# A gated pair of long convolutions on one core: gate sums in four column groups, eight unsummed Q rows, and the output stored in two parts

## The chip, the core and the metric

The kernel runs on one core of a Trainium2 chip. It uses five engines: TensorE (PE; its weight loads are listed apart as PEld), VectorE (DVE), ScalarE (ACT), GpSimd (POOL) and SyncE (SP), which here only issues transfers; ACT issues some too. The metric is device time in microseconds (us). Three timed runs of the kernel before gave 301.37, 303.55 and 303.87 us: a median of 303.55.

## The reference, cut to what matters

```python
x = A_u                                              # 2048 steps, 448 channels
g = sigmoid((x * gate_w).sum(-1, keepdims=True))     # one gate for each step
a = A_ref(x, A_re, A_im, B_re, B_im, C_re, C_im, log_dt, Dskip)
b = B_ref(x, k, v, shift_k, ssm_k, ssm_D)
return g * a + (1 - g) * b

# A: dt = exp(log_dt); K[d,l] = Re sum_n C[d,n] * exp(dt*A[d,n]*l) * dt*B[d,n], n < 256, l < 2048
#    y = causal convolution of x with K (by an FFT of length 4096) + x * Dskip
# B: kv = v * (k passed through a shift filter of 4 taps)
#    y = q * (causal convolution of kv with ssm_k + kv * ssm_D), with q = x
```

Inputs and output are bf16; both convolutions are per channel.

## The kernel before, in words

**Layout.** The 448 channels lie as 4 groups g of 112, the 2048 steps as 32 (a) by 64 (b). A natural tile such as `uu` (the input u), `vt`, `kt` or `ug` (the output) has 128 partitions (g, a) and 64 x 112 elements: partition 32g + a holds steps (a, b) of the channels of group g. The 112 channels are handled in 4 quarters H of 28 (`NC`), and each quarter of kernel generation in 2 blocks of 14 (`CB`), so 8 blocks j.

**Convolutions** are FFTs made of matmuls with generated twiddle tables: `spread` (first stage, PSUM tile `ps_c`, tables `Wc`, `WcK`), `transform` (second stage, `ps_2`, shown as `ps`, table `s_W`), a product in the frequency domain on DVE (`products`: `zs`, and the half-swapped copy `zsS`, which a DMA makes), then back by `stage_a` (`ps_a`, table `sa_R`) into `U` and by `stage_b` (`ps_b`, table `sb_G`). Between the stages ACT copies PSUM into SBUF (`evac`). The eight convolutions run in the order B0, B1, B2, A0, B3, A1, A2, A3.

**The SSM kernel K** is generated block by block (`KGen.block`, lines 398 to 464). exp(dt·A·l) with l = 8q' + ... is split into powers for Q rows (tile `kg_TQ`, 21 rows, `NQ`) and P columns (`kg_TP`, 32). Each level multiplies the rows it has by a unit phasor from table `ET`: `mult` makes the four real products of each complex multiplication into `kg_P4` (shown as `kg_P`) with one DVE instruction, and `add` sums them in pairs into `kg_TQ` or `kg_TP` with another. `pk` matmuls (224 for a block, in four column groups, weights `kg_TQ`, moving `kg_TP`) sum over the modes; ACT copies the result to `kg_S`; `ps_g` matmuls pick the right Q row for each l with 0/1 weights `ga_sel`, which `Consts.rows` and `Consts.gather` (lines 251 to 305) build from a table of row numbers; ACT copies the result to `kg_KT`, and `spread` takes it on. `kg_TQ` has two buffers, `kg_TP` one. Block 7's last products are done by halves (`transform_half`, `last`, `stage_a_half`).

**The gate.** `gwt` holds the gate weights, each times a 32-wide one-hot of the partition's a. 112 matmuls (line 917), one per channel of a group, add up into `ps_gate` (64 x 32): weights are `uu[:, :, l]` (128 x 64, stride 112), moving is `gwt[:, l, :]`. ACT copies the sums four times over into `gx`, PE transposes, ACT takes a tanh, DVE makes `gt` (g), `gb` (g in bf16) and `og` (1 − g).

**The end.** `mix` (line 867) scales the finished quarters of `ug` by 1 − g (`ug<-ug,og`) and of `uu`, which by then holds the A outputs (`uu<-uu,gb`), and adds them (`ug<-ug,uu`). For the last quarter `epilogue_A` multiplies each 16-b part of `ps_b` by g (`ept`), adds it to `ug`, and `store` (line 844) sends that quarter of b with all 112 channels to DRAM: 4 transfers, two on SP's queue and two on ACT's, 16 in all, each of 512 runs of 224 bytes.

**Order.** Nothing is scheduled by a planner's costs. Every instruction is first recorded (`Listed`, `Order`) and then issued in the order of the string `ORDER`, a list of record numbers; line 146 issues them all, so that the profile gives nearly every instruction line 146, and the groups are told apart by tile names. On each engine the instructions run in that order. Constants are carved from `scratch`, a tile that shares its buffer with `kg_TP`. Semaphores are added where one instruction needs another's result or buffer; transfers on the hardware queues take one of eight completion semaphores in turn, and an issue first waits for the earlier transfer with the same one.

Of the kernel before, what the change touches and what calls it, by code (L numbers as in the profile page):

```python
# [31 lines left out]
NQ = 21  # L32
# [9 lines left out]
    "600 25 576 30 164 1 190 525 24 36 188 196 162 189 175 177 23 34 186 191-192 187 176 193 526 534 26 31 552 173 "  # L42
    "171 580 174 536 581 0 32 160 593 537 2 166 172 528 33 73 535 598 21 179 17 35 540 11 10 14 3 22 28 75 16 6 182 "
    "178 13 18 12 29 15 7 19 198 184 9 38 591 8 5 20 4 37 181 74 65 180 183 39 76 201 27 161 550 197 577 168 200 167 "
    "41 542 163 544 589 169 165 194 79 590 40 582 170 541 195 42 599 583 52 199 185 202 586 592 69 584 587 585 588 "
    "100 46-47 203 50 72 51 553 44 595 204 594 551 43 538 48 45 110 66 49 557 68 77 101-108 90 53 78 55 554 71 56 539 "
    "150 54 596 63 556 111-118 67 109 62 597 70 527 91-98 555 80 61 64 119 529 140 531 151-158 99 530 234-241 602 545 "
    "130 141-148 159 242 215-222 543 532 120 149 225-232 548 205-212 223 233 213 267 214 549 243-250 224 252-259 547 "
    "251 81-88 533 546 260 121-128 89 319-326 129 262 268-283 261 327 131-138 284 264 263 285-300 139 266 302-317 265 "
    "301 575 516 499 318 493 1104 366 574 469 346-353 486 365 1106 1103 354 367 1105 471 502 470 364 474 473 472 468 "  # L50
    "481 370-385 490 573 477 570 498 562 578 507 567 489 513 561 482 560 494 815-830 483 512 478 579 479 495 484 487 "
    "491 496 488 480 492 485 503 603-616 521 497 522 504 1121 524 523 500 508 505 514 1108 617-630 501 509 517 1110 "
    "506 1109 631-644 510 518 1111 511 645-658 1119 558 1112 1122 1113 659-672 568 1117 673-686 572 559 1115 475 2483 "
    "687-700 566 515 563 1118 571 565 701-714 1124 831 1120 386 60 57-58 1126 798-813 1114 59 715 476 421-428 564 "
    "1123 716 814 1116 1107 1125 429 1510-1517 1846 717 1127 569 1476-1491 1518 2514 328-335 2498 1492 2515 781-796 "
    "519 1847 2497 2489 1848 718 404-419 2488 1129 520 720 1131 2487 719 1128 2491 2486 2492 2485 1133 797 1130 1132 "
    "420 1459-1474 1136 601 336 772-779 1135 1475 337-344 2490 1134 387-402 345 1137 2484 1849 832-839 780 1138 403 "
    "355-362 1850 840 1331-1362 1851 363 1267-1330 2499 1852 369 430-437 448-455 439-446 1853 368 1139-1202 1854 456 "
    "2518 2500 447 2519 1857 1203-1266 1856 2516 1855 438 946-953 2517 2509 1363 1860 1859 2510 1862 2511 1858 "
    "457-464 2520 755-770 2512 954 2521 1382-1421 2506 2502 465 1864 1493-1508 2505 2503 1422 1844 467 937-944 2507 "  # L60
    "1364-1380 1842 2504 1843 1381 1841 1509 1432-1439 2508 2538 2513 2494 721-736 2537 771 2493 2539 466 2495 "
    "738-753 737 754 2496 1639-1646 2533 2532 2540 2501 858-873 2558 2529 945 2528 2557 1861 1845 2522 901-908 2559 "
    "874 1863 1865 909 928-935 1867 1869 1647 2560 892-899 1871 936 2561 910-917 1866 900 919-926 918 1870 955-962 "
    "927 841-856 1868 2530 1872 1455 1648-1655 963 2563 1456 857 875-890 2531 2523 2565 1656 964-971 2524 2568 891 "
    "1873 1440 1038-1101 1874 2534 2525 1875 972 1441-1446 2535 1876 2552 1457 2069-2100 1877-1940 2544 2553-2554 "
    "2546 2005-2068 2549 1102 2545 2555 2550 1941-2004 2536 1458 2548 1447 2543 2541 2556 2551 3326 2547 1448-1453 "
    "2526 1613-1628 2542 2570-2571 2101 3328 3963 3327 2527 2573 1666-1673 1454 2562 1629 1657-1664 1423-1430 1674 "
    "2575 1579-1594 2564 1665 2566 1519-1534 2567 1595 3329 973-1036 3999 3966 3990 3965 3989 3970 3998 3330 3968 "
    "2569 3967 2197-2212 3972 1037 3964 1431 3971 2120-2159 2572 2213 1570-1577 6189 2160 1596-1611 1578 3331 1535 "
    "2102-2118 2574 1536-1551 3969 3333 2119 2577 1612 1630-1637 2186-2191 1552 2576 1553-1568 2579 1638 2578 "  # L70
    "2995-3002 1569 2585 2214-2229 3003 2193-2194 3332 2248-2255 2230-2246 2584 2256 1684-1691 3991 1711-1774 3334 "
    "2586 3335 2247 2581 1692-1700 3974 3973 2583 2192 2944-2959 1701 1775 2170-2178 1702-1709 2580 2960 2587 "
    "2161-2168 1675-1682 1710 3992 2961-2976 3336 1683 2582 3338 2716-2779 2977 3337 2196 2652-2715 2169 3975-3976 "
    "3985-3986 2195 2179-2184 3987 2588-2651 2185 2780-2811 3994 2812 2257-2272 3339 3995 3340 3996 3988 3342 3993 "
    "3978 4000 3344 3977 2317-2324 3350 2273 2335-2342 2813-2829 3979 4001 2308-2315 3983 2830 3352 2325 2831-2870 "
    "3341 4003 2316 3343 2915-2922 4004 2343 3345 2326-2333 3997 2871 1776-1839 3347 2334 3982 3349 3346 4005 2923 "
    "4013 3055-3062 4006 4002 2890-2895 1840 2291-2306 4007 3063 3351 6192 3984 2978-2993 3021-3036 2307 4018 4017 "
    "2994 2274-2289 4012 4019 3348 3037 3980 2924-2931 3353 3981 2344-2351 2290 3354 2352 3728-3735 3355 4029 4020 "
    "2904 2906-2913 3356 2905 4038 3549-3580 4037 4028 4008 4032 4039 4048 4026 3421-3484 4040 4021 4033 4009 4023 "
    "4041 3357-3420 4030 4042 4010 4044 3736 4046 3485-3548 2914 4047 4011 4014 4049 2418-2481 2932 4050-4051 4807 "  # L80
    "4806 4025 4053 4808 4055 4052 4022 4015 4031 2353-2416 4054 4016 2482 4036 4034 4027 4057 4024 3677-3692 3581 "
    "2896 2417 4035 5383 2933-2940 3693 4059 2897-2902 3038-3053 6195 2941 3711-3726 4065 2903 3054 3694-3709 2943 "
    "3727 2872-2879 5388 5392 5384 5393 5387 5406 2942 5386 5389 2880 5385 2881-2888 5391 5390 3710 5405 3115-3122 "
    "5394 4043 2889 3806-3813 5395 4809 3098-3113 4045 4810 4064 3600-3639 3123 3814-3822 5396 4066 3114 3081-3096 "
    "5418 4811 3640 3824-3831 3823 4056 3582-3598 4813 3097 3004-3019 4058 5419 3599 4060 3124-3131 4061 3832 "
    "3650-3657 3132 4062 3064-3079 4063 3658 4817 4067 3142-3149 5407 3666-3671 3080 4815 4132-4195 3672 5415 4816 "
    "3150 3641-3648 5414 4196-4259 4818 3649 5408 5416 4821 3020 5398 4823 5397 4825 5399 3659-3664 4260-4291 5417 "
    "3665 4068-4131 5400 4827 5401 5403 5402 4404-4411 4292 4820 4819 4822 5404 3169-3176 4412 4812 5420 4395-4402 "
    "4824 4293-4309 3177 4814 3151-3158 4826 4310 3133-3140 3159 4311-4350 4830 3141 3160-3167 5421 4351 4832 3673 "
    "3196-3259 3168 5428 5438 3674 5429 4403 5437 4828 5430 3178-3185 5439-5440 4377-4382 3260 4834 4475-4482 "  # L90
    "3186-3194 5458 5409 5424 5449 4833 3261-3324 4829 4835 5451 5455 4831 4836 5452 5456 5454 3195 5431 5029-5060 "
    "5423 5410 4965-5028 5444 3676 5442 5448 5443 3797-3804 3325 4901-4964 5453 6190 5447 5446 5445 5441 3675 5450 "
    "4727-4742 3805 5422 4837-4900 4384 4483 6191 5425 4458-4473 4385 5468 5844-5846 5471 5061 5457 5426 5411 "
    "3788-3795 5470 5459 4474 5473 5460 3796 3754-3769 5412 4383 5461 5413 5432-5433 4352-4359 5475 5427 5462 3770 "
    "4413-4421 5466 4386-4393 5464 4360 3737-3752 4394 5467 5847 4370-4375 5434 3771-3786 4423 3753 4376 4744-4759 "
    "3787 4422 4361-4368 4743 4710-4725 4760 3833-3896 5848 4726 5469 5435 5472 4369 4424-4439 3897 5463 4441-4456 "
    "4440 5474 5465 5062-5078 4535-4542 5436 5476 5079 4518-4533 5481 4543 4457 5080-5119 5478 4484-4499 5483 4534 "
    "5477 4544-4551 5120 4501-4516 4500 5479 5485 5121-5128 4552 4761-4768 4517 5484 3898-3961 4769 5480 5486 5129 "
# [60 lines left out]
class Consts:  # L159
# [31 lines left out]
    def onehot(self, name, n, col, scale=1.0, pool=None):  # L191
        t = (pool or self.pool).tile([P, n], f32, name=name)
        self.nc.vector.tensor_scalar(out=t[:], in0=self.iota(name + "_j", [[1, n]]), scalar1=col[:, 0:1],
                                     scalar2=scale, op0=ALU.is_equal, op1=ALU.mult)
        return t
# [788 lines left out]
```

## Time and profile before

| | |
|---|---|
| median of three runs | 303.55 us |
| profiled execution, its own time | 302.91 us |
| its span | 300.7 us |
| busy: PE, PEld | 224.0, 197.8 us |
| busy: DVE, ACT, POOL | 268.4, 257.7, 9.7 us |
| mean granted TensorE clock | 0.861 |
| last write of `kg_TP` (DVE) ends | 260.7 us |
| last `zs` product (DVE) ends | 282.0 us |
| last `ug` sum (DVE) ends | 290.8 us |
| packets moved by DMA | 53380, of which 48720 under 512 bytes |

Times inside the profile count from the span's start. A group line reads: source line, engine, operation, output<-inputs, partitions x elements, xcount | busy us, mean ns of one | idle time of the engine just before them, and what ended it. In the page's slices each digit is the busy share of a fortieth of the span in tenths, 9 being 90% or more. DVE instructions overlap a little, so that the time from one to the next is shorter than the duration of one.

### The profile page before, as it was taken

The page shows a single profiled execution, that of the slowest core. Times are in us where ns is not written, and L with a number is a line of the kernel's source. Part 1 is how long each engine was busy: PE and PEld are TensorE (multiplying, and loading weights), DVE is VectorE, ACT ScalarE, POOL GpSimd, SP SyncE. Part 2 cuts the span into 40 slices and gives each one's busy share as a digit, 9 for nine tenths or more (in the row PEclk, how much of TensorE's full clock was granted, in tenths as well). Part 3 has the DMA queues.
Part 4 walks back from the last instruction along what each step waited for, and adds up shares of the span by engine and source line. Part 5 has one row for each costly group of instructions (what it writes and reads, how often), then busy time and mean ns, then how long its engine had stood idle before and what let it go on. Part 6 is the DMA issues. An engine that isn't in the chain of part 4 may idle for free.

```text
span 300.7 us, 12051 instructions
## 1 busy us (share of the span) xinstructions
PE 224.0 (74%) x5386; PEld 197.8 (66%) x5386; DVE 268.4 (89%) x536; ACT 257.7 (86%) x413; POOL 9.7 (3%) x42
## 2 busy tenths in 40 slices
PE   0186664997956867998887696978869999869740
PEld 0033444996954766997777685867759988769730
DVE  8999999987987989899999999989999999983850
ACT  4899989979979999899799999999999999906600
POOL 6003000010000000000000000000000000000000
PEclk9999795557689797997999777999788999969995
DMA  6999999210234051040001410005050000900058
GB/s 126 185 216 168 175 154 282 43 23 0 49 80 63 0 125 50 2 104 25 5 2 34 95 49 2 2 5 121 7 124 2 2 4 20 220 17 4 3 112 134
DMA packets 53380, 21.34 MB, mean 71 GB/s; under 512 B 48720, under 2 KB 51664, under 8 KB 53328
## 3 DMA queue, kind: packets, MB, share of 16 engines
q1 hardware_dynamic: 48768, 19.42, 34.6%
q10 hardware_dynamic: 4560, 1.15, 2.0%
q8 instruction: 42, 0.69, 1.0%
q14 instruction: 10, 0.08, 0.1%
HBM read 10.01 MB, written 3.21 MB: 44 GB/s over the span
## 4 chain that ended last, share of the span: by engine, by line
ACT 34%; DVE 16%; PE 9%; issue 3%; DMA 2%; DVEq 0%; ACTq 0%; SPq 0%
ACT zs L146 13%; ACT ET L146 6%; ACT U L146 5%; ACT zsK L146 5%; DVE kg_P L146 4%; PE ps_a L146 3%; DVE kg_TP L146 3%; DMA zsS<-zs 2%; DVE zs L146 2%; ACT L146 2%; DVE ug L146 2%; DVE zsS L146 2%; PE ps_b L146 1%; PE ps_c L146 1%; PE pk L146 1%
## 5 line engine op out<-in xcount | busy, mean ns | idle before, releaser
L146 ACT CAST zs<-ps 128x896 bf16<-128x896 f32 x48 | 43.5, 935 | 1.2 <-PE ps L146 1.2
L146 DVE TENSOR_TENSOR kg_P<-kg_TQ,ET 128x896 bf16<-128x896 bf16 (+2 forms) x64 | 43.9, 705 | 0.6 <-ACT ET L146 0.4
L146 ACT CAST zs<-ps_c 128x1024 bf16<-128x1024 f32 (+1 forms) x48 | 42.4, 925 | 0.8 <-PE ps_c L146 0.8
L146 PEld LDWEIGHTS <-s_W 128*128 128x128 bf16 x544 | 32.7, 107 | 14.7 <-issue 12.2
L146 PE MATMUL ps_a<-sa_R,zs 128*128 128x128 bf16 x224 | 35.6, 245 | 5.0 <-ACT zs L146 3.6
L146 PE MATMUL ps<-zs,s_W 128*128 128x112 bf16 x384 | 30.0, 233 | 9.3 <-ACT zs L146 7.9
L146 PE MATMUL pk<-kg_TP,kg_TQ 128*21 128x32 bf16 x1792 | 30.9, 238 | 7.7 <-issue 5.1
L146 PE MATMUL ps_a<-sa_R,zsS 128*128 128x128 bf16 x224 | 34.9, 243 | 0.7 <-DVE zsS L146 0.7
L146 PEld LDWEIGHTS <-zsS 128*128 128x128 bf16 x224 | 30.8, 154 | 5.7 <-issue 4.2
L146 PEld LDWEIGHTS <-kg_TQ 128*21 128x21 bf16 x1792 | 27.8, 121 | 9.9 <-issue 8.3
L146 PE MATMUL ps_b<-U,sb_G 128*128 128x28 bf16 x1024 | 28.3, 176 | 6.1 <-ACT U L146 2.5
L146 DVE TENSOR_TENSOR kg_P<-kg_TP,ET 128x1792 bf16<-128x1792 bf16 (+1 forms) x32 | 30.7, 968 | 1.8 <-ACT ET L146 1.8
L146 PEld LDWEIGHTS <-sb_G 128*128 128x128 bf16 x1024 | 27.6, 97 | 7.1 <-issue 5.6
L146 PEld LDWEIGHTS <-zs 128*128 128x128 bf16 x224 | 30.7, 153 | 2.4 <-DVE zs L146 0.8
L146 ACT CAST U<-ps_a 128x1024 bf16<-128x1024 f32 (+2 forms) x30 | 28.3, 947 | 3.3 <-PE ps_a L146 3.2
L146 PEld LDWEIGHTS <-uu 128*64 128x64 bf16 x336 | 28.1, 212 | 3.4 <-DMA skraw<-in_B_ssm_k_dram 2.2
L146 DVE TENSOR_TENSOR kg_TQ<-kg_P 128x896 bf16<-128x896 bf16 (+2 forms) x64 | 27.3, 441 | 0.1
L146 ACT ACTIVATE ET<-ks_ph 128x448 bf16<-128x448 int16 x40 | 22.8, 595 | 1.6 <-DVE ks_ph L146 1.6
L146 PEld LDWEIGHTS <-scratch 128*128 128x128 bf16 x65 | 7.2, 112 | 25.0 <-DVE oA_f L146 10.8
L146 ACT ACT_TABLE_LOAD x15 | 19.2, 1283 | 4.3 <-DMA kt<-in_B_k_dram 4.0
L146 ACT CAST zsK<-ps_c 128x512 bf16<-128x512 f32 (+2 forms) x27 | 20.9, 779 | 0.7 <-PE ps_c L146 0.7
L146 DVE TENSOR_TENSOR kg_TP<-kg_P 128x896 bf16<-128x896 bf16 (+2 forms) x40 | 19.8, 500 | 0.0
(132 smaller groups left out, 455.5 us busy)
## 6 DMA issues: line engine op xcount, KB each, us to landing
zsS<-zs SPq DMA_DIRECT2D x16, 448.0 KB, 4.3
kt<-in_B_k_dram SPq DMA_DIRECT2D x16, 112.0 KB, 4.1
skraw<-in_B_ssm_k_dram SPq DMA_DIRECT2D x16, 112.0 KB, 4.4
vt<-in_B_v_dram SPq DMA_DIRECT2D x4, 448.0 KB, 7.1
uu<-in_A_u_dram SPq DMA_DIRECT2D x4, 448.0 KB, 5.9
xfd<-ks_hold SPq DMA_DIRECT2D x2, 672.0 KB, 6.2
ks_xf<-xfd SPq DMA_DIRECT2D x3, 336.0 KB, 2.9
out_dram<-ug SPq DMA_DIRECT2D x8, 112.0 KB, 4.7
```

Of the source, the lines that this page charges most:

```text
L146: ins = f(*args, **kw)
```

## The change

Five things are changed.

1. **Q rows of exponent 1.** The four rows that came from multiplying rows 0 to 3 by the phasor of exponent 1 are no longer summed. `leaf` writes the two products of each real and imaginary part into two rows of `kg_TQ` (rows 17 to 24), with two DVE instructions in place of one product and one sum. `kg_TQ` has 25 rows; the rows are renumbered, and `ga_sel` gets two ones where a row is a pair (`q_half`: the row number is replaced by min(q, (q + 17) >> 1)), so that the `ps_g` matmul adds the pair.
2. **Gate sums.** Weights and moving operand change places: weights `gwt[:, l, :]` (128 x 32), moving `uu[:, :, l]` (64 columns), in four column groups by l mod 4. A matmul with a 128 x 128 matrix of ones at equal a, in `gx`, adds the four groups and copies to all partitions, in place of the transpose.
3. **Stores.** At the end of `mix` the first 84 channels of each group are stored for all b: 4 transfers on SP's queue, each of 2048 runs of 168 bytes. The last epilogue stores the other 28 channels: 16 transfers as before, each of 512 runs of 56 bytes.
4. **Buffers.** Small constants that had tiles of their own are carved from `scratch`, and `ept` takes the buffer of `kg_KT`.
5. **`ORDER`** is a new list throughout, so instructions move on every engine.

```diff
-NQ = 21
+NQ = 25
...
 ORDER = (
-    "600 25 576 30 164 1 190 525 24 36 188 196 162 189 175 177 23 34 186 191-192 187 176 193 526 534 26 31 552 173 "
+    ...
...
+        def named(q):
+            return q if q < 4 else q + 13 if q < 8 else q - 4
...
+        def leaf(dst, src, e):
+            r, m = EQ[:, entry_of(e) + 1], src.shape[1]
+            for c in range(2):
+                V.tensor_tensor(out=TQ[:, dst + c:dst + c + 2 * m - 1:2], in0=src[:, :, c].unsqueeze(2).to_broadcast([P, m, 2, M]),
+                                in1=bass.AP(r.tensor, r.offset + c * M, [list(r.ap[0]), [0, m], [-M, 2], [1, M]]), op=ALU.mult)
...
-        q1 = mult([TQ[:, 0:4]], 1)
-        add(TQ, 8, q256)
-        add(TQ, 4, q1)
+        leaf(17, TQ[:, 0:4], 1)
+        add(TQ, 4, q256)
...
-    cons.gather(cons.field("q1", 0, 31), maskg)
+    q_col, q_half = cons.field("q1", 0, 31), cons.carve(1)
+    V.tensor_scalar(out=q_half, in0=cons.pidx[:], scalar1=31, scalar2=None, op0=ALU.bitwise_and)
+    V.tensor_scalar(out=q_half, in0=q_half, scalar1=17.0, scalar2=None, op0=ALU.add)
+    V.tensor_scalar(out=q_half, in0=q_half, scalar1=1, scalar2=None, op0=ALU.logical_shift_right)
+    V.tensor_tensor(out=q_col[:], in0=q_col[:], in1=q_half, op=ALU.min)
+    cons.gather(q_col, maskg)
...
-    def store(b0, n):
+    def store(b0, n, c0, c1, queues):
         for g in range(4):
-            dmae[g % 2].dma_start(out4[g][:, b0:b0 + n, :], ug[g * 32:(g + 1) * 32, b0:b0 + n, :])
+            queues[g % 2].dma_start(out4[g][:, b0:b0 + n, c0:c1], ug[g * 32:(g + 1) * 32, b0:b0 + n, c0:c1])
...
-            t = kgp.tile([P, 32, NC], bf16, name="ept")[:, 0:n]
+            t = kgp.tile([P, 32, NC], bf16, name="ept", tag="kg_KT")[:, 0:n]
...
-            store(b0, n)
+            store(b0, n, 3 * NC, 112, dmae)
...
                 V.tensor_tensor(out=o, in0=o, in1=x, op=ALU.add)
+        store(0, 64, 0, 3 * NC, (nc.sync, nc.sync))
...
-    V.tensor_copy(gx[:, 0:64], ident[:, 0:64])
+    V.tensor_scalar(out=gx[:, 64:192], in0=cons.iota("four_j", [[0, 4], [1, 32]]), scalar1=a1[:, 0:1], scalar2=None, op0=ALU.is_equal)
...
-        nc.tensor.matmul(pg[0:64, 0:32], lhsT=uu[:, :, l], rhs=gwt[:, l, :], start=(l == 0), stop=(l == 111))
-    nc.scalar.copy(gx[0:64, 64:192].rearrange("p (g a) -> p g a", g=4), pg[0:64, 0:32].unsqueeze(1).to_broadcast([64, 4, 32]))
-    nc.tensor.transpose(out=pg[:, 128:192], in_=gx[0:64, 64:192], identity=gx[0:64, 0:64])
+        q = 32 * (l % 4)
+        nc.tensor.matmul(pg[q:q + 32, 0:64], lhsT=gwt[:, l, :], rhs=uu[:, :, l], start=(l < 4), stop=(l >= 108), tile_position=(0, q))
+    nc.scalar.copy(gx[:, 0:64], pg[:, 0:64])
+    nc.tensor.matmul(pg[:, 128:192], lhsT=gx[:, 64:192], rhs=gx[:, 0:64], start=True, stop=True)
```

Counted from the two instruction lists: DVE has 8 products `kg_P<-kg_TQ,ET` of 128x1792 and 8 sums `kg_TQ<-kg_P` of 128x896 fewer, and 16 products `kg_TQ<-kg_TQ,ET` of 128x896 more. ACT has 13 table loads in place of 15. PE has as many matmuls as before. In the new order the halves of the last convolution stand differently on PE: the 28 `ps_a` matmuls of its first half, which stood ahead of the last `ps_c<-WcK`, stand at the end beside the 28 of the second; the `ps` matmuls of the first half, which stood ahead of the last `pk`, stand behind it. On DVE the last `uu<-uu,gb` and `ug<-ug,uu` stand ahead of the two `U` copies that precede the first `ept`.

## The prediction

> **What bounds the kernel now.** I read the busy shares first, then the 40 slices, then the stretches by engine, and last the end of the timeline. Busy shares and slices, from the page:
>
> ```profile
> span 300.7 us, 12051 instructions
> PE 224.0 (74%) x5386; PEld 197.8 (66%) x5386; DVE 268.4 (89%) x536; ACT 257.7 (86%) x413; POOL 9.7 (3%) x42
> DVE  8999999987987989899999999989999999983850
> ACT  4899989979979999899799999999999999906600
> DMA  6999999210234051040001410005050000900058
> ```
>
> Up to slice 35 (about 262 us) DVE and ACT are both nearly full: no engine alone is the bound, and a saving counts only as far as the other has one too. After that both have holes (a chain through PE), and the last slice and a half have no engine at all, only DMA. So I cost three pieces: the double-bound body up to the last write of `kg_TP` (DVE ends it at 260.7), the chain to the last output, and the stores.
>
> The body has one soft spot. Stretches of 2 us (columns: stretch, busy PE, PEld, DVE, ACT, POOL, granted clock, DMA):
>
> ```profile
> 62.00:64.00 2.00, 2.00 (x19) 2.00 (x18) 2.00 (x4) 1.28 (x2) 1.30 (x1) 0.50 0.00 0
> 64.00:66.00 2.00, 2.00 (x30) 2.00 (x30) 2.00 (x6) 0.83 (x3) 0.00 (x0) 0.50 0.00 0
> 66.00:68.00 2.00, 1.69 (x24) 1.47 (x23) 0.82 (x4) 1.85 (x5) 0.00 (x0) 0.50 0.05 12
> 68.00:70.00 2.00, 2.00 (x31) 1.66 (x26) 1.56 (x8) 1.73 (x4) 0.00 (x0) 0.50 0.00 0
> 70.00:72.00 2.00, 1.75 (x30) 1.63 (x28) 1.12 (x2) 2.00 (x8) 0.00 (x0) 0.91 0.00 0
> ```
>
> At a granted clock of 0.50 PE is full with the gate sums while ACT, and then DVE, stand still. Groups that the change touches (columns: busy, mean ns of one, idle before):
>
> ```profile
> L146 PE MATMUL ps_gate<-gwt,uu 128*64 128x32 bf16 x112 | 13.3, 277 | 2.0 <-ACT ET L146 2.0
> L146 PE MATMUL pk<-kg_TP,kg_TQ 128*21 128x32 bf16 x1792 | 30.9, 238 | 7.7 <-issue 5.1 <-DVE kg_TP L146 2.6
> L146 DVE TENSOR_TENSOR kg_P<-kg_TQ,ET 128x1792 bf16<-128x1792 bf16 x16 | 17.3, 1084 | 0.5 <-ACT ET L146 0.4
> L146 DVE TENSOR_TENSOR kg_TQ<-kg_P 128x896 bf16<-128x896 bf16 x24 | 14.6, 616 | 0.0
> L146 ACT ACT_TABLE_LOAD x15 | 19.2, 1283 | 4.3 <-DMA kt<-in_B_k_dram 4.0
> ```
>
> **Part 1, unsummed Q rows.** Each of 8 blocks loses one 128x1792 product and one 128x896 sum and gains two 128x896 products. Neighbouring DVE instructions overlap by about 0.08 us, so I take the pitch: 1.00 and 0.54 us. Saved: 8 × (1.00 + 0.54 − 2 × 0.54) = 3.7 us. The new products read runs of 112 elements; the sum row reads the same runs at 616 ns, so I give them its price. Bounds: nothing saved if one costs 0.77 us; at 1.00 us it is a loss of 3.7. The extra matmul columns (25 for 21) ride in weight loads: 21 columns cost 121 ns, 32 columns of `ga_sel` 99 ns, so nothing. Small constants on DVE: five more one-column instructions at 0.07 us and the new `gx` (0.15 for 0.20) cost +0.3 us, most of it before 12 us, where DVE is full. The saving reaches the body's end only if ACT gets shorter by as much; part 2 counts that.
>
> **Part 2, the new written order.** Counted from both instruction lists and priced by the rows of before: DVE has 246.2 us of work ahead of its last `kg_TP` write, and 242.6 after the change. ACT has 245.2 us ahead of its last `kg_S` copy, and 240.8: two table loads fewer (13 for 15, 2 × 1.28) and four 128x448 `zsK` copies (4 × 0.49) put behind it. DVE now idles 260.7 − 246.2 = 14.5 us up to that point. If that stays, the body is 3.6 us shorter, and ACT (−4.4) allows it. The order of every queue changes, so the idle time may move; the two lists put each block's `pk` within a few us of the same place in DVE's and ACT's work, so I keep 14.5, with ±2.
>
> **Part 3, gate sums.** 112 matmuls take 13.1 us (51.7 to 64.8), one each 0.118 us. After: weights 128x32 in four column groups, 64 moving columns. Bounds: the `pk` row in four groups runs 128 in 2.10 us (16 ns each, 32 moving columns), the `ps_c<-Wc,kv` row in two groups 32 in 2.24 us (70 ns, 128 moving), both at clock 0.50. So 1.8 to 7.8 us; I take 33 ns, twice `pk`, since the moving side doubles: 3.7 us. Either way the sums end before ACT has done the 23 `ET` pieces that stand ahead of the `gx` copy; ACT no longer waits 1.8 us there. Idle in 60–72 us is 2.7 us on DVE and 2.3 on ACT. What is late next is ACT's `ET` chain, whose exponents DVE awaits anyway, so I count half: −1.3 us (0 to −2.7).
>
> The `pk` row's 16 ns has weight loads and matmuls of different column groups overlapping over the same 128 rows. [...]
>
> **Part 4, stores.** The end of before (timeline; then the DMA share over the stretch):
>
> ```profile
> 284.67 1.08 DVE L146 TENSOR_TENSOR ug<-ug,uu 128x1792 bf16<-128x1792 bf16 x1
> ...
> 290.42 0.39 DVE L146 TENSOR_TENSOR ug<-ept,ug 128x448 bf16<-128x448 bf16 x1
> ```
>
> ```profile
> 287.37 8.53 SPq L146 DMA_DIRECT2D out_dram<-ug  x8
> ```
>
> ```profile
> 288.00:298.50 10.50, 0.67 (x27) 0.57 (x23) 2.50 (x6) 0.00 (x0) 0.00 (x0) 0.70 1.00 174
> 58.00:61.50 3.50, 3.50 (x32) 3.50 (x31) 3.30 (x7) 3.49 (x11) 0.00 (x0) 0.50 0.86 131
> ```
>
> The stores are bound by DMA: 8192 runs of 224 B fill 16 engines for 10.5 us, 20.5 ns a run. `skraw`, 3584 runs of 128 B, costs 0.86 × 3.5 × 16 / 3584 = 13.4 ns. The line through both gives 16.4 ns for 168 B and 8.1 for 56 B. The change makes **8192 early runs of 168 B and 8192 late ones of 56 B**: more DMA work, 12.5 us, so it gains only by starting early. But the early store waits for the last `ug<-ug,uu`, still almost the last thing before the final sums.
>
> Count from t0, the last `zs` product (282.04 before). Before: first `ept` at 4.3, data done at 16.5, span end at 18.7. After: DVE does `uu`, `ug` (2.2 us: early store issued), two `U` copies (2.2), `ps_b` (1.0): first `ept` at 5.4, last `ug` at 9.9. Early data start 0.9 later (issue 287.37, flow from about 288.2) and need 8.4, with the first late quarter's 1.0 between: the last early store lands at 2.2 + 0.9 + 9.4 + 0.6 = 13.1. **Added wait:** a DMA takes one of eight semaphores in turn and its issue waits for that semaphore's earlier user. By the instruction list the second late quarter waits for the early stores and the fourth for the second; queued behind are only further stores. At 2.7 us from issue to landing (small loads show 2.9, less run cost) quarter two's last lands at 15.8, quarter four's at 18.5, span end 1.6 later: 20.1, or +1.4. Ahead of t0, PE has 14 `ps_a` fewer (56 for 70) and 16 short `ps` more before `ps_c<-WcK`, which then starts about 1.0 earlier, and t0 comes 0.6 later after it: −0.4. Net **+1.0**. Ends: with 13.4 ns early and 5.1 late (by bytes) −1.8; with 20.5 for every run +5.8.
>
> [...] No run of this trace has 56 B.
>
> The `ept` tile shares `kg_KT`'s buffer; the last reader of that is `ps_c<-WcK`, 10 us before the first `ept`: nothing, and about 0.6 if it were not done.
>
> **Sum**, against the profiled run's own 302.91 (span 300.7 and 2.2 around it; the three timed runs have a median of 303.55, 0.6 above): 302.9 − 3.6 − 1.3 + 1.0 = **299.0**.
>
> **Rivals.**
> - *The small runs decide the tail* (slower). A 56 B write costs as much as a 224 B one, or more, and the chained quarters wait behind it: +5.8 in place of +1.0, 303.8; with no gate gain 305.1. It turns the sign once the tail costs over 4.9 us. For: the late quarters wait for the early ones. Against: 128 B runs cost a third less than 224 B. Chance 0.2.
> - *The new order stalls more* (the body does not shrink): DVE idles 18.5 instead of 14.5, 303.0. For: ACT has 85.4 us ahead of its first `kg_S`, 76.1 before, and `kg_TP` has one buffer. Against: the later blocks line up. Chance 0.16.
> - *Everything given* (faster): gate idle gone whole (−2.7), tail at its lower end (−1.8): 302.9 − 3.6 − 2.7 − 1.8 = 294.8. Chance 0.2.
> - *The products do not get cheaper*: 0.77 us for one of 128x896, 302.6. Chance 0.04, since the shape has rows.
>
> The forecast has 0.40. Its own width is ±2 (order) and the tail. The range takes the rivals' bodies: 294.5 to 305.2. A measurement of this kernel tells about 1% from no change (300.5 and 306.6 about the median): the forecast is mostly below 300.5, the fast rival wholly; of the slow tail a third lies above 306.6. Faster 0.54, same 0.31, slower 0.15.
>
> **What would show it.** `kg_TQ<-kg_TQ,ET` 128x896 x16 near 0.62 us; DVE busy near 265; 13 table loads; gate sums under 8 us; last `kg_TP` write near 256; then from the last `zs` product about 20 us to the span's end, early stores flowing some 3 us after it. A last `kg_TP` write after 259 makes the body wrong, a tail over 23 us the DMA price.

## The result and the profile after

| | before | after |
|---|---|---|
| median (lowest to highest), 4 runs each | 302.69 us (301.37 to 303.87) | 314.72 us (312.37 to 316.06) |
| profiled execution, its own time / span | 302.91 / 300.7 us | 314.24 / 312.3 us |
| last write of `kg_TP` ends | 260.7 | 259.8 |
| last `zs` product ends (t0) | 282.0 | 281.6 |
| last `ug` sum ends | 290.8 | 291.4 |
| from there to the span's end | 9.9 | 20.9 |

The change is **slower**: ratio 1.039, 95% interval 1.031 to 1.047. The forecast was 299.0, range 294.5 to 305.2. The table says where: the body is 0.9 us shorter, not 4.9, and the time behind the last `ug` sum has doubled. That last row alone is 11.0 of the 11.6 us by which the span grew.

The page of after, busy shares and slices:

```profile
span 312.3 us, 12060 instructions
PE 212.0 (68%) x5387; PEld 186.2 (60%) x5387; DVE 264.5 (85%) x540; ACT 255.6 (82%) x411; POOL 9.7 (3%) x43
DVE  8997999799999999989999995898599999088200
ACT  4999989999999999997999979999799693473000
DMA  7999997410810510130051005004100055004996
```

DVE's 3.9 us less work and ACT's 2.1 less are there. At the end ACT is empty for three slices and DVE for two, while DMA is busy up to the last. The tile views of `kg_TQ` and `ps_gate` (duration of one in ns as min/median/max, then first and last start) show that the two operations I had no row for came out as priced, 0.62 us for a product, and 112 gate sums in 3.6 us (51.2 to 54.8) where I had 3.7:

```profile
L147 DVE TENSOR_TENSOR kg_TQ<-kg_TQ,ET x16: 615/619/626, 63.5 to 245.8; 128x896 bf16<-128x896 bf16 x16
...
L147 PE MATMUL ps_gate<-uu,gwt x112: 278/302/309, 51.2 to 54.5; 128*32 128x64 bf16 x112
```

The end of after, stretches of 2 us (the last two columns are the mean busy share of the 16 DMA engines and GB/s):

```profile
286.00:288.00 2.00, 2.00 (x85) 2.00 (x83) 1.02 (x2) 0.00 (x0) 0.00 (x0) 1.00 0.85 139
...
290.00:292.00 2.00, 0.00 (x0) 0.00 (x0) 1.24 (x3) 0.00 (x0) 0.00 (x0) 0.50 1.38 104
...
298.00:300.00 2.00, 0.00 (x0) 0.00 (x0) 0.00 (x0) 0.00 (x0) 0.00 (x0) 0.50 1.85 65
...
302.00:304.00 2.00, 0.00 (x0) 0.00 (x0) 0.00 (x0) 0.00 (x0) 0.00 (x0) 0.50 0.44 27
...
306.00:308.00 2.00, 0.00 (x0) 0.00 (x0) 0.00 (x0) 0.00 (x0) 0.00 (x0) 0.50 1.60 26
```

Read the last two columns together. The share climbs from 0.85 to 1.85 while the rate falls, with ups and downs (119 at 296 to 298 us), from 139 to 65 and then 26 GB/s: the DMA engines are busier and move a fifth. Before, the same columns showed 1.0 with 174 GB/s. The dip at 302 us (0.44) is the chain of quarters, where an issue waits for an earlier transfer's semaphore (SP's queue waits 4.4 us for earlier stores, in three waits). So there were two suspects for the lost 11 us, the price of the runs and the chain; and a third question, why the body gave so little.

### The profile page after: what moved, and what is told of

It reads as the page before. It is cut to its first block, busy times and chain, and to the rows that moved or that the text cites. A ratio compares the mean times of both kernels' runs of the same rounds, so it can differ in the third digit from the quotient of the medians.

```text
span 312.3 us, 12060 instructions
## 1 busy us (share of the span) xinstructions
PE 212.0 (68%) x5387; PEld 186.2 (60%) x5387; DVE 264.5 (85%) x540; ACT 255.6 (82%) x411; POOL 9.7 (3%) x43
## 4 chain that ended last, share of the span: by engine, by line
ACT 32%; DVE 25%; PE 17%; SPq 10%; issue 6%; DMA 4%; DVEq 0%; ACTq 0%
ACT zs L147 12%; SPq L147 10%; ACT ET L147 9%; DVE kg_P L147 8%; PE pk L147 5%; ACT zsK L147 4%; DVE kg_TP L147 4%; PE ps_c L147 4%; PE ps_a L147 3%; PE ps L147 3%; DMA uu<-in_A_u_dram 3%; DVE kg_TQ L147 3%; ACT U L147 3%; DVE ug L147 2%; DVE zsS L147 2%
## 5 line engine op out<-in xcount | busy, mean ns | idle before, releaser
L147 PEld LDWEIGHTS <-s_W 128*128 128x128 bf16 x544 | 32.6, 108 | 17.6 <-issue 14.5
L147 PE MATMUL pk<-kg_TP,kg_TQ 128*25 128x32 bf16 x1792 | 31.3, 239 | 15.6 <-issue 13.1
L147 PEld LDWEIGHTS <-kg_TQ 128*25 128x25 bf16 x1792 | 28.0, 127 | 13.7 <-issue 12.1
L147 DVE TENSOR_TENSOR kg_P<-kg_TQ,ET 128x896 bf16<-128x896 bf16 (+2 forms) x56 | 36.0, 653 | 0.1
L147 PE MATMUL ps_a<-sa_R,zs 128*128 128x128 bf16 x224 | 33.9, 239 | 2.7 <-DVE zs L147 1.1
L147 PE MATMUL ps_a<-sa_R,zsS 128*128 128x128 bf16 x224 | 33.0, 236 | 1.0 <-DVE zsS L147 1.0
L147 PEld LDWEIGHTS <-zs 128*128 128x128 bf16 x224 | 29.9, 152 | 3.1 <-DVE zs L147 1.6
L147 DVE TENSOR_TENSOR kg_TQ<-kg_P 128x448 bf16<-128x448 bf16 (+2 forms) x56 | 23.3, 418 | 0.1
L147 DVE TENSOR_TENSOR kg_TP<-kg_P 128x896 bf16<-128x896 bf16 (+2 forms) x40 | 20.1, 504 | 3.2 <-PE pk L147 3.2
L147 PE MATMUL ps_c<-Wc,kv 128*64 128x128 bf16 x224 | 16.8, 303 | 8.7 <-ACT zs L147 7.5
L147 PEld LDWEIGHTS <-kv 128*64 128x64 bf16 x224 | 15.5, 219 | 9.5 <-issue 7.9
L147 PE MATMUL ps_v<-kvt,scratch 128*128 128x448 bf16 x64 | 16.3, 421 | 5.7 <-DVE kvt L147 4.5
```

Of the source, the lines that this page charges most:

```text
L147: ins = f(*args, **kw)
```

## The experiments on the stores

In all experiments "ratio" is against the kernel before in runs on the same chip, with its 95% interval; the kernel before had medians of 302.8 to 303.2. The experiments keep every instruction's place in the written order. To do so, `Order` has two helpers: `skip(n)` leaves n record numbers empty, and `attach(n)` issues the last n records right behind the record before them.

**The old store in the new kernel** (`t1_old_store`).

```diff
-            store(b0, n, 3 * NC, 112, dmae)
+            store(b0, n, 0, 112, dmae)
...
-        store(0, 64, 0, 3 * NC, (nc.sync, nc.sync))
+        nc.skip(4)
```

> The changed kernel with the store of before: sixteen transfers of all 112 channels (8,192 runs of 224 B), four behind each quarter, no early store; rows, gate and written order as changed. Theory S (the new store is the whole loss: from the last ug to the span's end 20.9 us after the change, 9.9 before): this gives back 11, 314.7 - 11 = 303.7, less than 1 us from the kernel before. Rival O (rows, gate and order cost too, for instance through the 13.1 us in which TensorE issues late behind the swaps): it stays 5 us or more above before, 308 or over. Rival G (the rows and the gate do give the 4.9 us that were foretold and the stores hide it): 298.

Measured: 303.08 us, ratio 1.002 (0.999 to 1.005); 9.8 us from the last `ug` sum to the span's end. Theory S holds: the store is the whole loss, and rows, gate and order together are worth nothing measurable.

**Chain or price?** `t2_late_once` sends the late channels once; `t4_late_only` leaves the early store out, so that 84 of the 112 channels of a group are not written.

```diff
 # t2_late_once
-            store(b0, n, 3 * NC, 112, dmae)
+            if b0 == 48:
+                store(0, 64, 3 * NC, 112, dmae)
+            else:
+                nc.skip(4)
```

```diff
 # t4_late_only
-        store(0, 64, 0, 3 * NC, (nc.sync, nc.sync))
+        nc.skip(4)
```

> The changed kernel with the early store as it is, but the 28 late channels leave once, behind the last quarter, in four transfers of 2,048 runs of 56 B, in place of four for each quarter. Number and length of the runs are the same; the chain of quarters that wait for each other and for the early store's completion is gone. Theory P (a run of 56 B costs 25 to 36 ns of a DMA engine, so 8,192 of them on 16 engines cost 13 to 18 us): now all of them lie behind the last ug, the end does not come sooner, 313 to 320. Theory C (the chain of waits costs it, the runs cost the 8 ns that I foretold): 8,192 x 8.1 / 16 = 4.1 us behind the last ug plus about 4 of a transfer's start and end, some 303.

> The changed kernel without the early store: 84 of the 112 channels of each group are left unwritten, the sixteen late transfers of 56-B runs stay. Theory P (the price of the late runs alone sets the end): the last quarters still end late, 308 or over. Theory B (the early store fills the DMA engines and the late ones wait behind it, as its 8,192 runs of 168 B at 19.5 ns need 10 us from 285 on): without it each quarter's 2,048 short runs go out between the quarters, and the last takes what the last quarter took before or less, 300 to 303.

Measured: `t2_late_once` 317.59, ratio 1.049 (1.042 to 1.056). The chain is gone, though all late runs now start behind the last `ug` sum too, and the kernel is slower still, 25.4 us behind that sum: theory C falls, the price stays. `t4_late_only` 305.02, ratio 1.007 (1.005 to 1.010), 13.4 us behind the last sum: between its two theories. With half of the changed kernel's runs and a quarter of its bytes, the late store alone issues its sixteen transfers from 286.1 to 296.5 us, and one takes 6.6 us from issue to landing (median); before issues its 224-B runs from 287.4 to 294.7 and takes 4.5. Not all of that is price: the last issue lies 7.0 us behind the last `ug` sum, 3.9 in before, which I read as the chain's wait for earlier stores. The experiments with one early store in four transfers, below, have no such chain.

**Shorter or cut?** `t3_runs_64` moves the split by four channels, from 84 to 80.

```diff
-            store(b0, n, 3 * NC, 112, dmae)
+            store(b0, n, 80, 112, dmae)
...
-        store(0, 64, 0, 3 * NC, (nc.sync, nc.sync))
+        store(0, 64, 0, 80, (nc.sync, nc.sync))
```

> The changed kernel with the split moved by four channels: 80 early and 32 late, so runs of 160 and 64 B in place of 168 and 56 B, as many as before. [...] Theory R (each run has its price whatever its length between 56 and 64 B): 314, within 1.5 us. Neither run's start then lies at a multiple of 64 B; if the start decides and not the length, it is as in theory R.

Measured: 305.25, ratio 1.009 (1.006 to 1.011). Eight bytes more in each late run give back 9.5 us, so theory R falls. (The expectation errs on the starts: a row of the output is 896 B, so half of the runs from byte 160 do begin at a multiple of 64 B.) Length under 64 B was now the obvious reading. Three more kernels test it; in `a1_56_at_160` the last four channels of each group are not written.

```diff
 # t5_half_early: channels 0 to 55 at once when they are done, 56 to 111 late
-            store(b0, n, 0, 112, dmae)
+            store(b0, n, 56, 112, dmae)
...
                 V.tensor_tensor(out=o, in0=o, in1=x, op=ALU.add)
+            if H == 1:
+                store(0, 64, 0, 56, (nc.sync, nc.sync))
+                nc.attach(4)
```

```diff
 # a1_56_at_160                                # a2_80_at_144
-        store(0, 64, 0, 3 * NC, ...)
+        store(0, 64, 0, 80, ...)              # 0, 72
-            store(b0, n, 3 * NC, 112, dmae)
+            store(b0, n, 80, 108, dmae)       # 72, 112
```

> The changed kernel with the old store (303.1), except that channels 0 to 55, which are finished at 265.9 with the second quarter's sum of ug and uu, leave right then in four transfers on SP (8,192 runs of 112 B), and the sixteen late transfers take channels 56 to 111 (112 B). Theory B (a run above 64 B is paid by its bytes: 224 B 20.5 ns, 160 B about 17, so 112 B about 13): the late quarter takes 1.7 us in place of 2.6 and the queue behind the last ug shrinks by 2 to 3 us, 300 to 301. Rival K (each run has one price, so twice the runs cost the same late and more early): 303. Rival Q2 (the early transfers, 7 us on all DMA engines from 266 on, hold up TensorE's instructions as the swaps seem to): 304 to 308.

> The changed kernel with runs of 160 B early (channels 0 to 79) and of 56 B late (channels 80 to 107), so that the short runs begin at byte 160 of the 224, a multiple of 32, and not at byte 168; channels 108 to 111 of each group are left unwritten. With 64 B from the same byte the kernel took 305.3, with 56 B from byte 168 it took 314.7. Half of the runs from byte 160 begin at a multiple of 64 B, as a row of four groups is 896 B. Theory L (what costs is a length under 64 B): 312 or more. Rival A (what costs is a start off the 32 B): 303 to 306. In between: both count.

> The changed kernel with the split at channel 72: 144 B early, 80 B late from byte 144. Nothing is left out. So far whole multiples of 32 B (224; 160 and 64) cost 303 and 305 in the changed kernel, while 112 and 112 (308.8), 160 and 56 (309.9) and 168 and 56 (314.7) end or begin inside a block of 32 B. Theory Z (each run that cuts a block of 32 B costs about 1.45 ns of the whole memory path, 8,192 of them 12 us: the early 112-B runs took 266 to 278.6, the late ones 290.5 to 302.7): here both the early and the late runs cut one, 16,384 of them, some 24 us from 284 on: 312 to 317. Theory L (only a length under 64 B is slow): 144 and 80 B are both longer, 303 to 306.

Measured: `t5_half_early` 308.79, ratio 1.022 (1.018 to 1.027); `a1_56_at_160` 309.86, ratio 1.023 (1.018 to 1.029); `a2_80_at_144` 318.01, ratio 1.050 (1.047 to 1.054). `t5_half_early` lies above all its theories, `a1_56_at_160` between its two. The last decides: 144 and 80 B are both longer than 64 B, and it is among the two slowest of all. Theory B (a price by bytes) and theory L (a length under 64 B) both fall; theory Z holds, a little above its 312 to 317. All nine kernels in one table; a run is **cut** if it begins or ends off a multiple of 32 B:

| kernel | early, late run (B) | cut runs | last `ug` sum to the end |
|---|---|---|---|
| before; old store in the new kernel | none, 224 | 0 | 9.9; 9.8 |
| `t3_runs_64` | 160, 64 | 0 | 12.3 |
| `t4_late_only` | none, 56 | 8,192 | 13.4 |
| `t5_half_early` | 112 (from 266 us on), 112 | 16,384, half of them long before the end | 13.7 |
| `a1_56_at_160` | 160, 56 | 8,192 | 16.6 |
| the change | 168, 56 | 16,384 | 20.9 |
| `a2_80_at_144` | 144, 80 | 16,384 | 25.3 |
| `t2_late_once` | 168, 56 | 16,384 | 25.4 |

That the block is 32 B, and not 16 or 64, follows from the same table, with addresses counted from the output's start: 112 and 144 B are multiples of 16 and their runs are slow, while every run of before cuts a block of 64 B (224 is three and a half of them) and none is slow. One cut end is enough: the early runs of `t5_half_early` and the late ones of `a1_56_at_160` begin on a block and only end off one.

The same number of runs, in four transfers on SP's queue each, shows the price without a chain (KB of one transfer, then median us from issue to landing): the 112-B runs of `t5_half_early` first, the 160-B runs of `t3_runs_64` second.

```profile
out_dram<-ug SPq DMA_DIRECT2D x4, 224.0 KB, 10.1
out_dram<-ug SPq DMA_DIRECT2D x4, 320.0 KB, 6.1
```

The change also takes longer after the last bytes have moved: from where the DMA share falls under 0.1 to the span's end it is 1.7 us in before (299.0 to 300.7) and 3.8 in the change (308.5 to 312.3), in half-us stretches. In `a2_80_at_144` the share is 0.01 or less from 312 us on, 3.7 us from the end.

The windows of `t5_half_early` show the price with nothing else in flight but instructions. First the stretches of its early store, of 112-B runs:

```profile
266.00:268.00 2.00, 2.00 (x32) 1.61 (x30) 0.00 (x0) 0.74 (x2) 0.00 (x0) 0.60 0.90 125
268.00:270.00 2.00, 2.00 (x44) 2.00 (x40) 0.00 (x0) 1.71 (x3) 0.00 (x0) 1.00 1.51 67
...
272.00:274.00 2.00, 1.40 (x44) 1.29 (x41) 1.88 (x3) 2.00 (x3) 0.00 (x0) 1.00 1.40 65
```

Then those of `t3_runs_64`, its early runs of 160 B and its last late ones of 64 B:

```profile
286.00:288.00 2.00, 1.99 (x76) 1.88 (x72) 1.72 (x5) 0.00 (x0) 0.00 (x0) 0.64 0.88 151
...
298.00:300.00 2.00, 0.00 (x0) 0.00 (x0) 0.00 (x0) 0.00 (x0) 0.00 (x0) 0.50 0.84 78
```

Cut runs start at 125 GB/s and after 2 us fall to 66, with a share of 1.4 to 1.5; the whole runs here hold their rate at a share under 1. (The share alone is no sign: the 224-B runs of before reach 1.33, at 195 GB/s.) At 66 GB/s a 112-B run takes 1.7 ns of all engines together, 27 ns of one. The 56-B runs of `t4_late_only` at their slow end (33 and 32 GB/s in the two stretches from 294 to 298 us) also take 1.7 ns, waits of the chain included. Whole runs take 0.8 ns (64 B, 78 GB/s) and 1.06 ns (160 B, 151 GB/s).

## The experiments on the body

**TensorE's stops.** The changed kernel had 13.1 us in which TensorE stood at `pk` with no wait that the profile shows ("issue"); before had 5.1. The four long stops (2.2, 1.9, 4.0 and 3.4 us) end 6 to 8 us after the issue of a half-swap `zsS<-zs`, whose transfers take 5.8 us to land (median); the other four swaps have no stop over 1.0 us at `pk` behind them. `f1_late_swap` is the changed kernel with the old store and moves the last swap of all, with the ACT copy that it waits for, behind the last `kg_S`:

```diff
 ORDER: ... 
-    "... 4801 ... 5807 ... 5808 ... 6104-6121 ..."
+    "... 6104 4801 5807-5808 6105-6121 ..."
```

> The changed kernel with the old store (303.1), and in the written order ScalarE's last copy of zs ahead of the last swap, with the swap's two transfers, moved behind the last kg_S. TensorE's own order is the same. With the old store the last pk sums stop for 3.7 us with no wait that the profile shows, from when the swap's 0.9 MB are on the DMA engines until 2 us after; kg_S and all that follows waits. Theory Q (TensorE's instructions come by DMA and queue behind the swap's bytes): the stop goes, kg_S is done 3 us earlier, the swap still lands ahead of its product at 274.6: 299.5 to 300.5. Rival W (the stop belongs to the pk sums or to TensorE's sequencer at this place): it stays, 303 to 304. Rival V (the stop only moves behind the later swap, to the next instructions that are fetched): 302 to 304, with a stop of 3 us among the ps_a or ps_g sums.

Measured: 302.32, ratio 0.997 (0.994 to 1.000). TensorE's timeline, `t1_old_store` first and `f1_late_swap` second (start, duration; in brackets the idle time before and its releaser):

```profile
260.05 2.87 PE L152 MATMUL pk<-kg_TP,kg_TQ 128*25 128x32 bf16 x176 [1.33 <-DVE kg_TP L152]
266.61 0.92 PE L152 MATMUL pk<-kg_TP,kg_TQ 128*25 128x32 bf16 x48 [3.70 <-issue]
```

```profile
259.32 2.87 PE L152 MATMUL pk<-kg_TP,kg_TQ 128*25 128x32 bf16 x176 [1.73 <-DVE kg_TP L152]
263.30 0.90 PE L152 MATMUL pk<-kg_TP,kg_TQ 128*25 128x32 bf16 x48 [1.10 <-issue]
```

The same 48 matmuls, in the same place of TensorE's order, stop for 1.10 us when no swap is in flight and for 3.70 when one is. Theory Q holds for the stop, and the stop of 3 us that rival V expects among the later sums is not in the trace: `kg_S` starts at 264.3 in place of 267.6. That it is TensorE's instructions which queue behind the swap is the reading that fits; no view ties a stop to one of their transfers. But only 1.1 us of the 3.3 reach the end: the swap's bytes now flow until 271, and the `zs` product, which overwrites what the swap reads, begins at 272.8 after DVE has stood for 3.5 us. (The profile puts that wait down to an ACT copy that ends just then; that it is the swap is argued.) A second sign is in `t5_half_early`: TensorE stops for 2.0 us of "issue" among the `ps_a` matmuls as its early store ends.

**Rows, gate and order apart.** Three kernels in the written order of before, with the stores of before (in it the two `leaf` products of a block stand where the product and the sum stood):

```diff
 # b1_rows_only: the changed kernel, but
-ORDER = ( ... after ... )
+ORDER = ( ... before ... )
-            store(b0, n, 3 * NC, 112, dmae)
+            store(b0, n, 0, 112, dmae)
-        store(0, 64, 0, 3 * NC, (nc.sync, nc.sync))
-        (the gate sums of after)
+        (the gate sums of before)
 # b2_gate_only: the kernel before, with the gate sums of after
 # b3_old_order: b1_rows_only, with the gate sums of after
```

> The kernel before with the unsummed rows and the buffers of the changed one alone: written order, stores and gate sums are those of before. DVE has 3.6 us less to do ahead of the last kg_TP. Theory D (my prediction: DVE's work sets when kg_TP is done and its idle time stays): 3.6 us faster, 299 to 300. Rival A (DVE and ScalarE are both nearly full up to there, 246 and 245 of 260 us, and wait for each other: with rows and gate together in this order the last kg_TP came 0.8 us sooner while DVE's idle time grew by as much as its work fell): 1 us faster or nothing, 302 to 303.

> The kernel before with the gate sums alone changed (u as the moving operand in four column groups; sums and the last product as after; written order, rows and stores of before). Theory G (my prediction: 13.1 us of TensorE become 3.7, and the 1.8 us in which ScalarE waits for them are given): 301 to 302, 1.3 us faster. Rival H (the sums lay beside other work, TensorE then waits for the next operand): 303, no change. With rows and gate in this order the whole was 0.5% faster, so rows and gate alone should add up to 1.4 us.

> The changed kernel with the rows, the gate sums and the buffers of after, but the stores and the written order of before (the eight leaf products and the new iota stand where the products and the gate's helpers stood). The changed kernel with the old store gave 303.1, no better than before, though DVE has 3.9 us less to do. Theory N (the new written order spends the gain: DVE's idle time ahead of the last kg_TP went from 14.5 to 17.2): in the old order the gain shows, 298 to 300. Rival M (it is not DVE's work that sets when kg_TP is done; waits on ScalarE and TensorE take up whatever DVE saves): 302 to 304, as with the new order. Rival X (the old order was fitted to the old lengths, and the new operations stall in it): 304 or more.

| | median | ratio |
|---|---|---|
| `b1_rows_only` | 305.56 | 1.009 (1.006 to 1.012) |
| `b2_gate_only` | 299.48 | 0.990 (0.986 to 0.994) |
| `b3_old_order`: both | 301.46 | 0.995 (0.993 to 0.998) |
| `t1_old_store`: both, in the new order | 303.08 | 1.002 (0.999 to 1.005) |

The gate sums alone give 3 us, more than theory G had. The rows, which do take 3.6 us from DVE, cost 1.6 (beside the gate, where the two intervals just touch) to 2.8 (alone): theories D and A both fall, since neither expected a loss. Both together, in the old order, come out between theory N and rival M. The new order costs another 2.

**Why the rows give nothing.** Two more kernels, each with one suspect:

```diff
 # x1_copies_to_dve: b3_old_order, and in Order.issue
+MOVED = (1381, 2119, 2871, 3599, 4351, 5120)
...
+                    if n in MOVED:
+                        f = self.tc.nc.vector.tensor_copy
```

```diff
 # b4_buffers_only: the kernel before, and
-        ti = self.pool.tile([P, 1], i32, name=name + "_i")
+        ti = self.carve(1)
...
-            t = kgp.tile([P, 32, NC], bf16, name="ept")[:, 0:n]
+            t = kgp.tile([P, 32, NC], bf16, name="ept", tag="kg_KT")[:, 0:n]
```

> The changed kernel's rows and gate in the written order and with the stores of before (301.5, 0.5% faster than before), and of the two copies of kg_KT out of ps_g in each of blocks 1 to 6 one is made by DVE in place of ScalarE, in the same place of the order: ScalarE gives 6 x 0.55 = 3.3 us, DVE takes 6 x 0.62 = 3.7, as much as the rows gave it. Theory A (ScalarE sets the pace from 160 to 240 us, where it is busy 19.9 of every 20; the rows were no gain because they took work from DVE alone): 2 to 3 us faster than without the move, 298.5 to 299.5. Rival D (DVE sets it): 2 to 4 us slower, 303 to 305. Rival E (the two, or TensorE, wait for each other by turns): within 1 us.

> The kernel before with the buffers of the changed one alone: small fields and one-hot tiles carved from the scratch tile, ept in the buffers of kg_KT. Rows, gate, order and stores are those of before. Theory B (the rows' 0.9% loss is the buffers': constants in the scratch tile, which is a buffer of kg_TP, or ept waiting for a kg_KT to come free): 305, 2 to 3 us slower. Rival R (the loss is the rows' own, by the eight products or the 25 rows that stay alive): 302.5 to 303.5, no change.

Measured: `x1_copies_to_dve` 300.88, ratio 0.995 (0.992 to 0.997), just what `b3_old_order` had; `b4_buffers_only` 302.90, ratio 1.000 (0.998 to 1.003). So the buffers are innocent, and neither engine alone is the bound: with the work handed from ACT to DVE, 3.3 us less for ACT give nothing, as 3.6 less for DVE did (rival E). The trace shows one place where time goes. In `b3_old_order` the stretch from the second `kg_S` to the third takes 31.5 us where `b2_gate_only` takes 29.7, and from there on the stretches agree within 0.5: nothing of DVE's saving shows in any of them. (From the first to the second it is 31.7 for 30.3, but `c3_gate_whole_32` below, which has no such rows, also has 31.7 there.) In the longer stretch stand these two lines, of DVE's and of ACT's timeline:

```profile
134.80 0.62 DVE L151 TENSOR_TENSOR kg_TQ<-kg_TQ,ET 128x896 bf16<-128x896 bf16 x1 [2.49 <-ACT ET L151]
...
145.21 0.58 ACT L151 ACTIVATE ET<-ks_ph 128x448 bf16<-128x448 int16 x1 [2.41 <-DVE ks_ph L151]
```

DVE stands for 2.5 us at a leaf product for a phasor that ACT has still to write, and 10 us later ACT stands for 2.4 us for phases that DVE has still to write. Each engine runs its list in order, so I read it thus: time saved on one turns into a wait for the other, and the wait is handed back. All five kernels with the rows in this order (`b1_rows_only`, `b3_old_order`, `x1_copies_to_dve` and, from below, `c2_whole_32` and `c4_copies_whole_32`) have both waits, and their stretch takes 30.2 to 31.5 us; the four without the rows (before, `b4_buffers_only`, `b2_gate_only`, `c3_gate_whole_32`) have neither, and theirs takes 29.2 to 29.9. That goes together; no run takes away the waits alone. And it is not the whole loss: in `b1_rows_only` the stretch is only 0.3 us longer than before, and its profiled execution, at 302.5, was the quickest of eleven, so its trace doesn't show what makes it 305.6 in the middle. That stays open.

**Better than both kernels.** Runs of whole 32-B blocks allow an early store: 48 channels are 96 B, the other 64 are 128 B, and the first two quarters (56 channels) are done near 266 us. `c2_whole_32` has it on `b3_old_order`, `c3_gate_whole_32` on `b2_gate_only`, `c4_copies_whole_32` on `x1_copies_to_dve`:

```diff
-            store(b0, n, 0, 112, dmae)
+            store(b0, n, 48, 112, dmae)
...
                 V.tensor_tensor(out=o, in0=o, in1=x, op=ALU.add)
+            if H == 1:
+                store(0, 64, 0, 48, (nc.sync, nc.sync))
+                nc.attach(4)
```

> The changed kernel's rows and gate sums in the written order of before, and an early store that cuts no block of 32 B and leaves while the DMA engines have nothing to do: channels 0 to 47 (96 B) right behind the second quarter's sum of ug and uu, near 268, and channels 48 to 111 (128 B) in the sixteen late transfers. Without the early store this kernel took 301.5. Theory Z (whole blocks are paid by bytes and runs, about 14 ns for 128 B in place of 20.5): the stores behind the last ug shrink by 2 us, 299 to 300. Rival L (all short runs are slow): 306 or more. Rival Q (the early store, 7 us on the DMA engines, holds up TensorE's instructions by 2 us, as the early store of 112-B runs did): 301 to 303.

> The kernel before with the gate sums changed (alone 1.0% faster) and the early store of 96 B runs, late runs of 128 B, no row change. If the two gains add (1.0% and the 0.6% between the kernels with rows and gate without and with this store): 297.5 to 298.5. If the early store and the earlier end collide (its bytes hold up TensorE's instructions): 299 to 300.

> Rows, gate, the six copies of kg_KT on DVE, and the early store of whole 32-B blocks, all in the written order of before. Theory A: below the kernel with rows, gate and that store (299.6) by 2 to 3 us, 296.5 to 297.5. Rivals D and E: 299.5 or more.

| | median | ratio | last `ug` sum to the end |
|---|---|---|---|
| `c2_whole_32` | 299.61 | 0.989 (0.986 to 0.992) | 7.5 |
| `c3_gate_whole_32` | **297.56** | 0.983 (0.978 to 0.987) | 8.0 |
| `c4_copies_whole_32` | 298.83 | 0.988 (0.985 to 0.992) | 7.5 |

The store gives about 2 us in each of the three pairs (301.46 to 299.61, 299.48 to 297.56, 300.88 to 298.83). The two parts' gains add, as the expectation for `c3_gate_whole_32` had it, and `c4_copies_whole_32`, whose ratio is that of `c2_whole_32` within the intervals, shows nothing of theory A's 2 to 3 us. The late runs of 128 B in `c3_gate_whole_32`:

```profile
288.00:290.00 2.00, 0.00 (x0) 0.00 (x0) 0.00 (x0) 0.00 (x0) 0.00 (x0) 0.50 1.07 152
290.00:292.00 2.00, 0.00 (x0) 0.00 (x0) 0.00 (x0) 0.00 (x0) 0.00 (x0) 0.50 1.36 148
```

150 GB/s is 0.85 ns a run, 14 ns of one engine. The best kernel is the change's second part alone with its third part recut: 1.7% faster than before, 5.5% faster than the change.

## Why the prediction was wrong

Of the 15 us between the forecast and the profiled run of after, about 11 lie in the tail (part 4) and 4 in the body (parts 1 to 3).

- **Part 4, the price line: the step that failed.** I drew a line through 224 B (20.5 ns) and 128 B (13.4) and read 168 B at 16.4 and 56 B at 8.1 ns. That made 12.5 us of DMA work; the two stores flowed for 24 (284.5 to 308.3). The 112-B runs of `t5_half_early` and the 56-B runs of `t4_late_only` took 27 ns of an engine at their slow rate. Both points of the line were runs of whole 32-B blocks, and the second was a load besides, so the line said nothing of stores that cut a block, as both new lengths do. The chain's term was too small with it: 2.7 us from issue to landing for a late transfer, where the median was 5.4 on ACT's queue and 6.8 on SP's. The times up to the last `ug` sum were right to 0.1 us: early store issued 2.2 us after t0 (2.2), first `ept` at 5.3 (5.4), last `ug` at 9.8 (9.9). Then the end came at 30.7, where I had 20.1, beyond the 23 that I had named as the sign of a wrong DMA price.
- **The added wait**, the chain of semaphores, was real (the dip at 302 us) and was not the main cost: without it, `t2_late_once` took longer. How much of the 11 us it holds, no run parts.
- **The first rival** ("the small runs decide the tail") was nearest, at a chance of 0.2, with the price of 20.5 ns a run, which I gave as the upper end, +5.8 us. It measured +12.0 (30.7 from t0 to the span's end, 18.7 before). Its reason was not the right one: whole runs of 64 B are small too and take 0.8 ns of all engines, cut runs of 112 B take 1.7. An end taken from the longest run of the trace is no bound for a kind of run that the trace doesn't have.
- **Part 1** was right in its size (0.62 us for a product, 3.9 us less DVE) and wrong in its worth. I wrote that a saving counts only as far as the other engine has one too, and then let it count whole because ACT lost 4.4. "If that stays", of DVE's 14.5 us idle, was the step that failed: it became 17.2 (259.8 less 242.6). In the old order the rows are a loss, and `x1_copies_to_dve`, which lightens ACT but gives DVE its work back, gains nothing either. No run in the old order lightens both.
- **Part 2** had 13 table loads right. The second rival, the order that stalls more, came true beside the first: the new order costs 2 us (1.002 to 0.995). The "issue" at `pk` goes with it, 13.1 us in the change and 5.5 in `b3_old_order`; that it is the cause is not shown.
- **Part 3** had the sums right: the 112 matmuls over the same rows, with their 112 weight loads (3.3 us busy), took 3.6 us in all, 32 ns each, against 118 before. Their worth was mis-sized the other way: I counted −1.3 with −2.7 as the end, and alone they gave 3.3 (302.76 to 299.48). In its trace the first `kg_S` comes 1.2 us sooner than before and the third 4.0 (1.3 and 3.2 in `c3_gate_whole_32`), so more than half of the gain arises behind the stretch that I priced, 60 to 72 us. How it does stays open. Nor was that stretch read right: the sums of before end at 64.8 us, so DVE's idle time from 66 on lies behind them and not beside them.

## What to carry to other kernels

Before a row of the output is split between two transfers, look at where each run begins and ends in bytes: in these runs cuts at a multiple of 32 B cost about what their bytes and count say (8,192 runs of 96 B flowed for 8.5 us, of 224 B for 10.5); any other cut made 8,192 runs of 112 B flow for 12 us, and 16,384 runs of 168 and 56 or of 144 and 80 B for 24 to 28 us, so 12 to 14 us for 8,192 at either length. A price line from a trace holds for runs of the same kind only. And in a list where two engines in turn wait for each other, less work on one is worth nothing until a run shows it: measure each part alone before adding them up.

## What the runs showed of the hardware

- **Cut runs.** 8,192 cut runs of 112 B take about 12 us (`t5_half_early` from 266 to 278), 1.5 ns each, against 8.5 us for 8,192 whole ones of 96 B (`c3_gate_whole_32` from 268 to 276.5) and 10.5 for those of 224 B. The mark in the profile is a DMA share that rises while GB/s falls: in `t5_half_early` to 1.15 to 1.51 at 65 to 67 GB/s, behind a first 2 us of 0.90 at 125, in the change from 0.85 at 139 to 1.85 at 65. Source and target are cut alike here (a partition's row is 224 B too), so the runs don't tell which side it is.
- **Stops behind data.** TensorE stops with no wait shown while or just after large transfers are in flight: 3.70 us at the same 48 matmuls behind a swap, 1.10 without. The reading that fits is that instructions (0.69 MB in all, on a DMA queue of their own, `q8` of the page) come late behind the data; it is argued, not shown.
